# Attention products that read each 128-column tile's two halves alternately, in a fused attention, MoE and GLU kernel

## The chip, the cores and the metric

The kernel runs on one core of a Trainium2 chip. The metric is the device time of one execution in microseconds (us), from the first to the last instruction with what lies around it. The program is one launch: bucketed attention, a top-1 mixture of experts and a gated linear unit follow each other on the same core.

## The reference

Sixteen attention heads (2 batches of 8) have 768 rows of 64 numbers each. A row's bucket is the six signs of its product with `proj`; a query sees only keys of its own bucket.

```python
q_bits = (np.einsum('bhsd,dk->bhsk', q, proj) > 0)      # k_bits likewise; buckets from the bits
mask = q_bucket[:, :, :, None] == k_bucket[:, :, None, :]
scores = np.where(mask, scale * np.matmul(q, k.transpose(0, 1, 3, 2)), -1e9)
attn = np.exp(scores - scores.max(-1, keepdims=True))
out = np.matmul(attn / (attn.sum(-1, keepdims=True) + 1e-9), v)
...
# MoE: each of 1536 rows goes to its best of 8 experts: gate * (relu(x @ w1[e]) @ w2[e])
# GLU: RMS norm, then (silu(xn @ w_gate) * (xn @ w_val)) @ w_out
```

Softmax sums and maxima over keys don't depend on the order in which the keys stand, as long as `v` has the same order. That is what the change uses.

## The kernel before

**Numbers.** Float32 operands are split into a high part `hi` and a rest `lo`, both in a reduced float32 type that TensorE multiplies in one pass. A product is then two or three matmuls into the same PSUM bank.

**Head preparation** (`prep_head`). A head's k and q lie side by side in `kq`, 128 partitions of 6 rows each. Three transposes (`wf`, L501) at a time give 384 columns, from which ScalarE writes `kqh` (L503) and VectorE `kql` (L504). Three sign products (`wp`, L531 to L533) of 384 columns follow; VectorE turns their signs into rows `ft` (L538), and DMAs of the SP queue (`moves`, L495, and L541, L542) put the pieces into the operands `kA`, `kB`, `qA`, `qB`. `kqh` and `kql` exist once (KQ = 1), so that the next head's must wait until these DMAs have read the last head's.

**Units.** A head has 6 units of 128 queries, 96 units in all, numbered `u`. For each unit: `scores` makes `S` (128 queries by 768 keys) in four matmuls of 384 columns (L550, L551); VectorE takes the row maximum (`neg`, L555, and `negm`, L560); ScalarE the exponentials `P` (L569); six transposes put `P` into PSUM tiles `T` (L588, two tiles of 384 columns); ScalarE writes its high part `pth` (L597) and VectorE its rest `ptl` (L598). After three units, `av` multiplies their 384 columns with `v`, 12 matmuls in all (`O`, L619 to L622), spread over the next group's units. `O` is copied out by ScalarE (`osb`, L639) and transposed back by small matmuls (`wo`, L654).

**Order.** The order of the steps is written out by hand: a string of letters (`ORDER`), one letter a step, is run once for each unit; each engine then takes its own instructions in that order. In it `scores(u+2)` comes ahead of `transposes(u)` and of the `av` products, `maxima(u+2)` comes ahead of the two `ptl` of unit `u`. `T`, `wf` and `wp` share three PSUM banks (WB = 3) in turn, `S` has two pairs of banks.

**Reading order.** In the MoE and GLU stages the moving operand of a matmul (the one whose columns stream through the array) is read through `turns`: column 0 of the first half, column 0 of the second half, column 1 of the first, and so on. What is written from those products is sorted back, or their inputs were stored in halves. In attention the moving operand is read column after column. I call these reads turned and plain.

**Loads.** `load_head` issues one DMA for k and one for q from the SP queue (head 0: two each, q's from ScalarE's queue).

Of the kernel before, what the change touches and what calls it, by code (L numbers as in the profile page):

```python
# [14 lines left out]
ALU = mybir.AluOpType  # L15
# [4 lines left out]
P = 128  # L20
# [24 lines left out]
def turns(t):  # L45

    return t.rearrange("p (h a) -> p a h", h=2)


def halves(t):  # L50
# [10 lines left out]
def lsh_attention_moe_glu(  # L61
# [15 lines left out]
    nc = tc.nc  # L77
    B, H, S, D = q.shape
# [5 lines left out]
    T = S // P  # L84
# [3 lines left out]
    HW = 3 * P  # L88
# [113 lines left out]
    for e in range(E):  # L202
        for w_, a_ in ((moe_w1[e], KC), (moe_w2[e], 2)):
            for f in range(F1 // W):
                s_ = w_[:, f * W:(f + 1) * W] if a_ == KC else w_[f * W:(f + 1) * W, :]
# [3 lines left out]
    for f in range(F2 // W):  # L209
        for w_ in (moe2_w_gate, moe2_w_val):  # L210
            s_ = w_.bitcast(I32)[:, 2 * f * W:2 * (f + 1) * W].rearrange("(c p) f -> p c f", p=P)
# [113 lines left out]
    with ExitStack() as ac:  # L325
# [5 lines left out]
        def load_head(n):  # L331
            if n >= NH:
                return
            b, h = divmod(n, H)
            kq = ld.tile([P, T, 2 * D], F32, tag="kq", name=f"kq{n}")
            for j in range(2 if n == 0 else 1):
                ts = slice(3 * j, 3 * j + 3) if n == 0 else slice(0, T)
                for i, src in enumerate((k, q)):
                    eng = nc.scalar if n == 0 and i == 1 else nc.sync
                    eng.dma_start(kq[:, ts, i * D:(i + 1) * D], src[b, h].rearrange("(p t) d -> p t d", t=T)[:, ts])  # L340
            if n == 0:
                for rs in (slice(0, D), slice(D, 2 * D)):
                    nc.sync.dma_start(pr[rs], proj)
            raw[n] = [kq]
            if n != 1:
                load_v(n)
# [83 lines left out]
        vst = {}  # L430
# [39 lines left out]
        def prep_head(n, banks=("w",)):  # L470


            if n >= NH:
                return
            kq = raw[n][0]
            hi = sp.tile([P, S], F32R, tag="kqh", name=f"kqh{n}", bufs=KQ)
            lo = sp.tile([P, S], F32R, tag="kql", name=f"kql{n}", bufs=KQ)
            ft = sp.tile([P, S], F32R, tag="ft", name=f"ft{n}", bufs=1)[0:F]
            bank = {"w": (ps_w, "w"), "0": (ps_w, "w"), "1": (ps_w, "w"), "O": (ps_o, "O")}
            ws = [bank[banks[i % len(banks)]] for i in range(4)]  # L480

            def places():
                for lst, nm in ((kB, "kB"), (qB, "qB")):
                    lst[n] = sp.tile([P, S], F32R, tag=nm, name=f"{nm}{n}")
                for lst, nm in ((kA, "kA"), (qA, "qA")):
                    lst[n] = sp.tile([D + 2 * NB, S], F32R, tag=nm, name=f"{nm}{n}")

            def moves():
                if n > 0:
                    places()  # L490
                lst = [(qA[n][0:D], hi[D:2 * D]), (kB[n][D:2 * D], lo[0:D]), (qB[n][0:D], lo[D:2 * D])]
                if n > 0:
                    lst += [(kA[n][0:D], hi[0:D]), (kB[n][0:D], hi[0:D]), (qB[n][D:2 * D], hi[D:2 * D])]
                for dst, src in lst:
                    nc.sync.dma_start(dst.bitcast(F32), src.bitcast(F32))  # L495

            for j in range(2):
                cs = slice(j * HW, (j + 1) * HW)
                w = ws[j][0].tile([P, 512], F32, tag=ws[j][1], name=f"wf{n}{j}")
                for i in range(3):  # L500
                    nc.tensor.transpose(w[:, i * P:(i + 1) * P], kq[:, 3 * j + i, :], ident)  # L501
                yield
                nc.scalar.activation(hi[:, cs], w[:, 0:HW], AF.Copy, scale=scv)  # L503
                nc.vector.scalar_tensor_tensor(lo[:, cs], w[:, 0:HW], scv, hi[:, cs].bitcast(F32), ALU.mult, ALU.subtract)  # L504
                if n == 0:
                    if j == 0:
                        places()
                    nc.scalar.copy(qB[n][D:2 * D, cs], hi[D:2 * D, cs].bitcast(F32))
                    nc.gpsimd.tensor_scalar(kB[n][0:D, cs], hi[0:D, cs].bitcast(F32), 1.0, 0.0, ALU.mult, ALU.add)
                    if j == 1:  # L510
                        nc.scalar.copy(kA[n][0:D], hi[0:D].bitcast(F32))
                if j == 1 and n < ML:
                    moves()
                yield
            if n == 0:

                rs = slice(D, D + 2 * NB)
                for i, (bk, dst) in enumerate((("1", kA[n]), ("O", kA[n]), ("w", qA[n]), ("0", qA[n]))):
                    j, c0 = i % 2, i // 2 * 32
                    cs = slice(j * HW, (j + 1) * HW)  # L520
                    w = bank[bk][0].tile([P, 512], F32, tag=bank[bk][1], name=f"wp{n}{i}")
                    for i_, (hl, src) in enumerate((("h", hi), ("l", hi), ("h", lo))):
                        nc.tensor.matmul(w[0:rs.stop, 0:HW], pw[hl][:, c0:c0 + rs.stop], src[:, cs], start=i_ == 0, stop=i_ == 2)
                    nc.vector.tensor_scalar(dst[rs, cs], w[rs, 0:HW], 0.0, gam0[rs, i // 2:i // 2 + 1], ALU.is_gt, ALU.subtract)
                    if i < 2:
                        nc.gpsimd.tensor_scalar(dst[rs, cs], dst[rs, cs].bitcast(F32), BIG, 0.0, ALU.mult, ALU.add)
                return
            for j in range(2):
                cs = slice(j * HW, (j + 1) * HW)
                w = ws[2 + j][0].tile([P, 512], F32, tag=ws[2 + j][1], name=f"wp{n}{j}")  # L530
                nc.tensor.matmul(w[0:F, 0:HW], pw["h"][:, D:], hi[:, cs], start=True, stop=False)  # L531
                nc.tensor.matmul(w[0:F, 0:HW], pw["l"][:, D:], hi[:, cs], start=False, stop=False)
                nc.tensor.matmul(w[0:F, 0:HW], pw["h"][:, D:], lo[:, cs], start=False, stop=True)  # L533
                yield
                if j == 0 and n >= ML:

                    moves()
                nc.vector.tensor_scalar(ft[:, cs], w[0:F, 0:HW], 0.0, gam, ALU.is_gt, ALU.subtract)  # L538
                nc.gpsimd.tensor_scalar(ft[0:2 * NB, cs], ft[0:2 * NB, cs].bitcast(F32), BIG, 0.0, ALU.mult, ALU.add)
                if j == 1:  # L540
                    nc.sync.dma_start(qA[n][D:D + 2 * NB].bitcast(F32), ft[32:F].bitcast(F32))  # L541
                    nc.sync.dma_start(kA[n][D:D + 2 * NB].bitcast(F32), ft[0:2 * NB].bitcast(F32))  # L542
                yield

        def scores(u):
            n, t = unit(u)
            s_ = ps_s.tile([P, 2, 512], F32, tag="S", name=f"S{u}")
            for j in range(2):
                cs = slice(j * HW, (j + 1) * HW)
                nc.tensor.matmul(s_[:, j, 0:HW], qA[n][:, t * P:(t + 1) * P], kA[n][:, cs], start=True, stop=False)  # L550
                nc.tensor.matmul(s_[:, j, 0:HW], qB[n][:, t * P:(t + 1) * P], kB[n][:, cs], start=False, stop=True)  # L551
            St[u] = s_

        def maxima(u):
# [47 lines left out]
        def av(g, chunks, t0=0, tn=3):  # L602

            n = order[g][0]
            if tn == 1:

                if t0 == 0:
                    spare.append(ps_s.tile([P, 2, 512], F32, tag="S", name="spare"))
                    Ob[g, t0] = spare[0][:, 0]
                else:  # L610
                    Ob[g, t0] = ps_w.tile([P, 512], F32, tag="w", name=f"O{g}{t0}")
            elif (g, t0) not in Ob:
                Ob[g, t0] = ps_o.tile([P, 512], F32, tag="O", name=f"O{g}")
            hi, lo = PT[g]
            cs = slice(t0 * P, (t0 + tn) * P)
            o = Ob[g, t0]
            for c in chunks:
                if c == 0:
                    nc.tensor.matmul(o[:, cs], vst[n][:, c, :], hi[:, c, cs], start=True, stop=False)  # L619
                nc.tensor.matmul(o[0:D, cs], vst[n][:, c, 0:D], lo[:, c, cs], start=False, stop=False)  # L620
                if c > 0:
                    nc.tensor.matmul(o[:, cs], vst[n][:, c, :], hi[:, c, cs], start=False, stop=c == T - 1)  # L622
            if T - 1 in chunks:
                done.append((g, t0, tn))
                if t0 + tn == 3:
                    PT.pop(g)

        def keep():

            if done:  # L630
# [5 lines left out]
                    o = ld.tile([P, T, 2 * D], F32, tag="kq", name="osbl")[:, 0]  # L636
                else:
                    o = sp.tile([P, HW], F32, tag="osb", name=f"osb{g}{t0}")[:, 0:tn * P]
                nc.scalar.copy(o, Ob.pop((g, t0))[:, t0 * P:(t0 + tn) * P])  # L639
                backs.append(give_back(g, t0, tn, o))  # L640

        def give_back(g, t0, tn, o):
# [711 lines left out]
```

## Time and profile before

| | |
|---|---|
| median of 3 runs | 751.41 us (749.9 to 751.46) |
| the profiled execution's own time | 750.34 us |
| its span, first to last instruction | 748.7 us |
| TensorE busy | 727.0 us, 97% |
| VectorE busy | 596.2 us, 80% |
| ScalarE busy | 375.5 us, 50% |
| GpSimd busy | 256.2 us, 34% |
| attention / MoE / GLU, from their matmuls' starts | to about 271, to about 459, to the end |

An engine is busy while an instruction of its own runs. TensorE's matmuls overlap, and their ends are modelled: a matmul's duration there holds a fixed part of some 0.16 us that the next one hides. What a matmul costs in a stream is therefore read from the distance between two starts, not from its duration.

### The profile page before, as it was taken

How to read it: one execution, taken by the hardware profiler on the slowest of the kernel's cores; microseconds unless marked ns; L12 is line 12 of the kernel's file. 1: busy time of each engine (PE TensorE's matmuls, PEld its weight loads, DVE VectorE, ACT ScalarE, POOL GpSimd, SP SyncE). 2: the span in 40 equal slices, each digit the busy share in tenths (PEclk: the TensorE clock that was granted, in tenths of full speed). 3: DMA queues.
4: the chain of work that ended last, by engine and by line, in shares of the span. 5: the costliest groups of instructions: out<-in, count | busy, mean ns of one | idle time of the engine just before them, and what ended most of it. 6: DMA issues, size and time to landing. Idle time of an engine off the chain costs nothing.

```text
span 748.7 us, 12565 instructions
## 1 busy us (share of the span) xinstructions
PE 727.0 (97%) x4459; PEld 658.1 (88%) x4460; DVE 596.2 (80%) x1094; ACT 375.5 (50%) x777; POOL 256.2 (34%) x434
## 2 busy tenths in 40 slices
PE   8999999999999989999999999999999999999996
PEld 7899999999999889999889888888888888888885
DVE  6999999999999758888798967865777777777633
ACT  5788888888898734345433454433222122211210
POOL 5143444436635543234263422221121121211124
PEclk9999999999999999999999999999999999999999
DMA  7799956555742147577778685422122122210012
GB/s 180 160 267 241 225 133 153 130 146 167 186 108 68 44 131 250 157 228 267 223 229 246 192 281 162 131 59 82 56 57 85 56 62 81 58 56 1 0 57 112
DMA packets 80546, 103.44 MB, mean 138 GB/s; under 512 B 31799, under 2 KB 50231, under 8 KB 80480
## 3 DMA queue, kind: packets, MB, share of 16 engines
q1 hardware_dynamic: 76480, 92.95, 45.1%
q0 software_dynamic: 3200, 9.46, 3.4%
q8 instruction: 36, 0.59, 0.3%
q10 hardware_dynamic: 800, 0.20, 0.1%
q14 instruction: 30, 0.25, 0.1%
HBM read 69.53 MB, written 14.72 MB: 113 GB/s over the span
## 4 chain that ended last, share of the span: by engine, by line
PE 73%; DVE 10%; DMA 4%; issue 4%; ACT 4%; POOL 2%; SPq 1%; POOLq 0%; DVEq 0%; ACTq 0%
PE T L588 8%; DVE lo L275 5%; PE O L620 4%; PE S L550 4%; PE S L551 4%; PE O L622 4%; PE z L1298 4%; PE z L1300 4%; PE z L1299 4%; PE pg L1275 4%; PE pv L1275 4%; PE pg L1276 4%; PE pv L1276 4%; PE pv L1277 4%; PE pg L1277 4%
## 5 line engine op out<-in xcount | busy, mean ns | idle before, releaser
L320 POOL TENSOR_TENSOR wa<-wa,hi 128x512 f32<-128x512 f32 x36 | 58.3, 1619 | 215.4 <-ACT hi L316 209.0
L316 ACT CAST hi<-wa 128x512 fp32r<-128x512 f32 x36 | 22.3, 620 | 162.1 <-DVE wa L314 155.1
L569 ACT ACTIVATE P<-S,negm 128x768 f32<-128x768 f32 x96 | 95.9, 999 | 7.9 <-DVE negm L560 7.1
L598 DVE TENSOR_TENSOR ptl<-T,pth 128x384 fp32r<-128x384 f32 x192 | 97.5, 548 | 1.1 <-ACT pth L597 1.0
L555 DVE TENSOR_REDUCE neg<-S 128x1 f32<-128x768 f32 x96 | 91.0, 948 | 7.8 <-PE S L551 7.3
L597 ACT CAST pth<-T 128x384 fp32r<-128x384 f32 x192 | 82.9, 488 | 7.5 <-PE T L588 5.1
L275 DVE TENSOR_TENSOR lo<-raw,hi 128x1024 fp32r<-128x1024 f32 x58 | 83.8, 1478 | 2.2 <-POOL hi L274 2.2
L588 PE MATMUL T<-ident,P 128*128 128x128 f32 x576 | 79.7, 273 | 0.6 <-ACT rkc L745 0.3
L588 PEld LDWEIGHTS T<-ident,P 128*128 128x128 f32 x576 | 68.6, 141 | 5.4 <-DVE ptl L598 1.4
L550 PE MATMUL S<-kA,qA 76*128 76x384 f32 x192 | 68.3, 356 | 1.9 <-ACT kqh L503 1.3
L551 PE MATMUL S<-kB,qB 128*128 128x384 f32 x192 | 65.3, 340 | 0.4 <-DMA qB<-kql 0.4
L1206 PE MATMUL ph<-xTh,lo 128*128 128x256 f32 x224 | 61.7, 275 | 1.2 <-DVE lo L275 1.2
L1204 PE MATMUL ph<-xTh,hi 128*128 128x256 f32 x224 | 62.8, 280 | 0.0
L620 PE MATMUL O<-ptl,vst 128*64 128x384 f32 (+1 forms) x198 | 62.0, 342 | 0.0
L1205 PE MATMUL ph<-xTl,hi 128*128 128x256 f32 x224 | 61.6, 275 | 0.0
L1280 DVE TENSOR_TENSOR sg<-pv,sg 128x512 f32<-128x512 f32 x36 | 24.7, 686 | 40.6 <-PE pv L1277 40.6
L1275 PE MATMUL pg<-gxh,hi 128*128 128x512 f32 x144 | 54.7, 380 | 0.0
L1298 PE MATMUL z<-hi,hi 128*128 128x512 f32 x144 | 54.7, 380 | 0.0
L1276 PE MATMUL pg<-gxl,hi 128*128 128x512 f32 x144 | 54.6, 379 | 0.0
L1277 PE MATMUL pg<-gxh,lo 128*128 128x512 f32 x144 | 54.6, 379 | 0.0
L1275 PE MATMUL pv<-gxh,hi 128*128 128x512 f32 x144 | 54.6, 379 | 0.0
L1276 PE MATMUL pv<-gxl,hi 128*128 128x512 f32 x144 | 54.6, 379 | 0.0
(236 smaller groups left out, 1952.5 us busy)
## 6 DMA issues: line engine op xcount, KB each, us to landing
raw<-in_moe_w_dram SPq DMA_DIRECT2D x64, 512.0 KB
raw<-in_moe_w_gate_dram SPq DMA_DIRECT2D x12, 512.0 KB
raw<-in_moe_w_val_dram SPq DMA_DIRECT2D x12, 512.0 KB
raw<-in_moe_w_out_dram SPq DMA_DIRECT2D x12, 512.0 KB
xs<-fill SPq DMA_DIRECT2D x16, 257.0 KB
xw<-xs SPq DMA_DIRECT2D x7, 514.0 KB
yt<-yd SPq DMA_DIRECT2D x12, 256.5 KB
v<-in_v_dram SPq DMA_DIRECT2D x16, 192.0 KB
```

The source lines that it names most:

```text
L275: pending.append((i, lambda: (nc.vector.tensor_tensor(lo, r, hi.bitcast(F32), ALU.subtract), load_next())))
L550: nc.tensor.matmul(s_[:, j, 0:HW], qA[n][:, t * P:(t + 1) * P], kA[n][:, cs], start=True, stop=False)
L551: nc.tensor.matmul(s_[:, j, 0:HW], qB[n][:, t * P:(t + 1) * P], kB[n][:, cs], start=False, stop=True)
L555: nc.vector.tensor_reduce(neg[u % 4][:, 1:2], St[u][:, :, 0:HW], AX.XY, ALU.max, negate=True)
L569: nc.scalar.activation(p_, St.pop(u)[:, :, 0:HW], AF.Exp, bias=nm[:, 1:2], scale=nm[:, 0:1], accum_out=sums[n][:, t:t + 1])
L588: nc.tensor.transpose(w[:, c * P:(c + 1) * P], p_[:, j, c * P:(c + 1) * P], ident)
L598: nc.vector.tensor_tensor(lo[:, 3 * j:3 * j + 3, cs], wv, hi[:, 3 * j:3 * j + 3, cs].bitcast(F32), ALU.subtract)
L620: nc.tensor.matmul(o[0:D, cs], vst[n][:, c, 0:D], lo[:, c, cs], start=False, stop=False)
L1275: nc.tensor.matmul(ps_, wh[:, c, fs], turns(xTh[b][:, c]), start=c == 0, stop=False)
L1276: nc.tensor.matmul(ps_, wh[:, c, fs], turns(xTl[b][:, c]), start=False, stop=False)
L1277: nc.tensor.matmul(ps_, wl[:, c, fs], turns(xTh[b][:, c]), start=False, stop=c == KC - 1)
L1298: nc.tensor.matmul(z, hi[:, s_, ts_], turns(oh_[:, s_]), start=s_ == 0, stop=False)
```

## The change

The moving operands of the scores, of the sign products and of the weighted values are read turned within each tile of 128 columns: column `a` of the first 64, then column `a` of the second 64. For the weighted values the columns are queries, so the copy to `osb` sorts them back (it reads PSUM at every second column). For the scores the columns are keys: `S`, `P` and `T` then hold the keys in turned order, and so that this is `v`'s order, k's even rows are loaded into partitions 0 to 63 and its odd rows into 64 to 127, by two DMAs of 64 partitions instead of one of 128. The signs of the sign products are sorted as they are written.

```diff
+def turns_by_tile(t):
+    return t.rearrange("p (c h a) -> p c a h", h=2, a=P // 2)
+def tiles_halves(t):
+    return t.rearrange("p (c h a) -> p c h a", h=2, a=P // 2)
+def tiles_sorted(t):
+    return t.rearrange("p (c a h) -> p c h a", h=2, a=P // 2)
...
                     eng = nc.scalar if n == 0 and i == 1 else nc.sync
+                    if i == 0:
+                        rows = src[b, h].rearrange("(a r t) d -> r a t d", r=2, t=T)
+                        for r in range(2):
+                            eng.dma_start(kq[r * (P // 2):(r + 1) * (P // 2), ts, 0:D], rows[r][:, ts])
+                        continue
                     eng.dma_start(kq[:, ts, i * D:(i + 1) * D], src[b, h].rearrange("(p t) d -> p t d", t=T)[:, ts])
...
-                nc.tensor.matmul(w[0:F, 0:HW], pw["h"][:, D:], hi[:, cs], start=True, stop=False)
+                nc.tensor.matmul(w[0:F, 0:HW], pw["h"][:, D:], turns_by_tile(hi[:, cs]), start=True, stop=False)
...
-                nc.vector.tensor_scalar(ft[:, cs], w[0:F, 0:HW], 0.0, gam, ALU.is_gt, ALU.subtract)
+                nc.vector.tensor_scalar(tiles_halves(ft[:, cs]), tiles_sorted(w[0:F, 0:HW]), 0.0, gam, ALU.is_gt, ALU.subtract)
...
-                nc.tensor.matmul(s_[:, j, 0:HW], qA[n][:, t * P:(t + 1) * P], kA[n][:, cs], start=True, stop=False)
-                nc.tensor.matmul(s_[:, j, 0:HW], qB[n][:, t * P:(t + 1) * P], kB[n][:, cs], start=False, stop=True)
+                nc.tensor.matmul(s_[:, j, 0:HW], qA[n][:, t * P:(t + 1) * P], turns_by_tile(kA[n][:, cs]), start=True, stop=False)
+                nc.tensor.matmul(s_[:, j, 0:HW], qB[n][:, t * P:(t + 1) * P], turns_by_tile(kB[n][:, cs]), start=False, stop=True)
...
-                nc.tensor.matmul(o[0:D, cs], vst[n][:, c, 0:D], lo[:, c, cs], start=False, stop=False)
+                nc.tensor.matmul(o[0:D, cs], vst[n][:, c, 0:D], turns_by_tile(lo[:, c, cs]), start=False, stop=False)
...
-                nc.scalar.copy(o, Ob.pop((g, t0))[:, t0 * P:(t0 + tn) * P])
+                nc.scalar.copy(tiles_halves(o), tiles_sorted(Ob.pop((g, t0))[:, t0 * P:(t0 + tn) * P]))
```

On TensorE, VectorE, ScalarE and GpSimd every instruction keeps its place; only the SP queue gets new rows. Here is the SP queue from the program's start to the end of head 1's moves, before (names are tile<-source; the L numbers are lines of the kernel of before):

```order
L340 DMA kq_93<-in_k_dram 128x3x64 x2
L343 DMA pr<-in_proj_dram 64x6 x2
L351 DMA v_100<-in_v_dram 128x384
L340 DMA kq_164<-in_k_dram 128x6x64
L340 DMA kq_164<-in_q_dram 128x6x64
L495 DMA qA_204<-kqh_192 64x768
L495 DMA kB_201<-kql_193 64x768
L495 DMA qB_202<-kql_193 64x768
L351 DMA v_278<-in_v_dram 128x384
L896 DMA wd<-in_moe_w_gate_dram 64x8x8 x2
L340 DMA kq_285<-in_k_dram 128x6x64
L340 DMA kq_285<-in_q_dram 128x6x64
```

And the same place of the SP queue with the change (its lines are numbered 17 to 19 higher):

```order
L357 DMA kq_93<-in_k_dram 64x3x64 x4
L362 DMA pr<-in_proj_dram 64x6 x2
L370 DMA v_102<-in_v_dram 128x384
L357 DMA kq_166<-in_k_dram 64x6x64 x2
L359 DMA kq_166<-in_q_dram 128x6x64
L514 DMA qA_207<-kqh_195 64x768
L514 DMA kB_204<-kql_196 64x768
L514 DMA qB_205<-kql_196 64x768
L370 DMA v_281<-in_v_dram 128x384
L915 DMA wd<-in_moe_w_gate_dram 64x8x8 x2
L357 DMA kq_288<-in_k_dram 64x6x64 x2
L359 DMA kq_288<-in_q_dram 128x6x64
```

Head 0's k takes two issues more ahead of `proj`, each later head's k one more, and everything behind them in the queue comes that much later.

## Rows read from the trace of the kernel before

**Rows 1.** Windows: PE, PEld, DVE, ACT, POOL busy (count), granted clock, DMA share, GB/s.

```profile
30.00:240.00 210.00, 210.00 (x1481) 196.58 (x1480) 200.59 (x427) 184.26 (x412) 96.95 (x224) 1.00 0.68 171
```

**Rows 2.** Chain of waits from 150 to 175 us, shares by engine and line.

```profile
by line: PE T L588 25.8%; PE S L550 14.5%; PE S L551 14.2%; PE O L620 13.3%; PE O L622 11.3%; PE wo L654 7.5%; PE wp L531 2.8%; PE wp L533 2.8%; PE wp L532 2.7%; PE wf L501 2.6%; PE O L619 2.2%; PE wk L739 0.4%; PE wk L740 0.2%; PE wk L737 
```

**Rows 3.** Timeline of TensorE, plain reads of 384 columns: start, duration, what.

```profile
155.64 0.34 PE L550 MATMUL S<-kA,qA 76*128 76x384 f32 x1
...
156.35 0.82 PE L588 MATMUL T<-ident,P 128*128 128x128 f32 x6
...
157.18 0.33 PE L622 MATMUL O<-pth,vst 128*128 128x384 f32 x1
...
157.87 0.34 PE L622 MATMUL O<-pth,vst 128*128 128x384 f32 x1
```

**Rows 4.** The same view in the GLU stage, turned reads of 512 columns.

```profile
650.00 0.38 PE L1275 MATMUL pg<-gxh,hi 128*128 128x512 f32 x1
...
653.02 0.38 PE L1277 MATMUL pv<-gxh,lo 128*128 128x512 f32 x1
```

**Rows 5.** The same view, 256 columns: plain at 267 us, turned at 276 us.

```profile
267.14 0.40 PE L857 MATMUL xacc<-hot,xl 128*128 128x256 f32 x2
267.38 0.39 PE L857 MATMUL xacc<-hot,ftx 128*128 128x256 f32 x2
...
275.88 0.28 PE L1204 MATMUL ph<-xfhi,hi 128*128 128x256 f32 x1
...
276.88 0.28 PE L1204 MATMUL ph<-xfhi,hi 128*128 128x256 f32 x1
```

**Rows 6.** Groups by line and shape on TensorE: count, busy us, mean ns, idle before.

```profile
L550 PE MATMUL S<-kA,qA 76*128 76x384 f32 x192 | 68.3, 356 | 1.9 <-ACT kqh L503 1.3 <-ACT P L569 0.5
...
L620 PE MATMUL O<-ptl,vst 128*64 128x384 f32 x186 | 60.1, 350 | 0.0
```

**Rows 7.** Timeline of TensorE: one unit's scores, and those six units later.

```profile
114.26 0.42 PE L550 MATMUL S<-kA,qA 76*128 76x384 f32 x1
...
129.61 0.42 PE L550 MATMUL S<-kA,qA 76*128 76x384 f32 x1
```

**Rows 8.** Timeline of VectorE in one unit.

```profile
153.80 0.60 DVE L538 TENSOR_SCALAR ft<-wp,gam 44x384 fp32r<-44x384 f32 x1
154.33 0.94 DVE L555 TENSOR_REDUCE neg<-S 128x1 f32<-128x768 f32 x1
...
155.30 0.16 DVE L560 SCALAR_TENSOR_TENSOR negm<-neg 128x2 f32<-128x2 f32 x1
155.38 1.02 DVE L598 TENSOR_TENSOR ptl<-T,pth 128x384 fp32r<-128x384 f32 x2
```

**Rows 9.** Timelines of VectorE and TensorE where a transpose follows closely on `ptl`.

```profile
160.11 1.02 DVE L598 TENSOR_TENSOR ptl<-T,pth 128x384 fp32r<-128x384 f32 x2
...
161.06 0.82 PE L588 MATMUL T<-ident,P 128*128 128x128 f32 x6
```

**Rows 10.** Groups on ScalarE and VectorE that read PSUM sorted (L1302, L1167) and plain.

```profile
L1279 ACT ACTIVATE sg<-pg 128x512 f32<-128x512 f32 x36 | 21.3, 593 | 19.2 <-PE pg L1277 19.2
...
L1302 ACT COPY acc<-z 128x512 f32<-128x512 f32 x12 | 7.0, 586 | 5.3 <-PE z L1300 5.3
...
L1211 DVE SCALAR_TENSOR_TENSOR hl<-ph,hh 128x512 fp32r<-128x512 f32 x32 | 21.8, 685 | 16.3 <-ACT hh L1210 16.3
...
L1167 DVE TENSOR_TENSOR xTl<-wxw,xTh 128x512 fp32r<-128x512 f32 x14 | 9.6, 687 | 5.6 <-ACT xTh L1166 5.6
```

**Rows 11.** Timeline of the SP queue at the start: start, us of the issue, what.

```profile
4.40 0.65 SPq L340 DMA_DIRECT2D kq<-in_q_dram  x1
6.58 0.54 SPq L495 DMA_DIRECT2D qA<-kqh  x1
```

**Rows 12.** Chain of waits from 20 to 60 us: start, us, what.

```profile
17.14 6.53 DMA qB<-kqh
...
23.74 0.59 ACT kqh L503
```

More of the change, by code (lines that the diff above doesn't have):

```diff
@@ L522, in prep_head @@
                     for i_, (hl, src) in enumerate((("h", hi), ("l", hi), ("h", lo))):
-                        nc.tensor.matmul(w[0:rs.stop, 0:HW], pw[hl][:, c0:c0 + rs.stop], src[:, cs], start=i_ == 0, stop=i_ == 2)
-                    nc.vector.tensor_scalar(dst[rs, cs], w[rs, 0:HW], 0.0, gam0[rs, i // 2:i // 2 + 1], ALU.is_gt, ALU.subtract)
+                        nc.tensor.matmul(w[0:rs.stop, 0:HW], pw[hl][:, c0:c0 + rs.stop], turns_by_tile(src[:, cs]), start=i_ == 0, stop=i_ == 2)
+                    nc.vector.tensor_scalar(tiles_halves(dst[rs, cs]), tiles_sorted(w[rs, 0:HW]), 0.0, gam0[rs, i // 2:i // 2 + 1], ALU.is_gt, ALU.subtract)
                     if i < 2:
@@ L530, in prep_head @@
                 w = ws[2 + j][0].tile([P, 512], F32, tag=ws[2 + j][1], name=f"wp{n}{j}")
-                nc.tensor.matmul(w[0:F, 0:HW], pw["h"][:, D:], hi[:, cs], start=True, stop=False)
-                nc.tensor.matmul(w[0:F, 0:HW], pw["l"][:, D:], hi[:, cs], start=False, stop=False)
-                nc.tensor.matmul(w[0:F, 0:HW], pw["h"][:, D:], lo[:, cs], start=False, stop=True)
+                nc.tensor.matmul(w[0:F, 0:HW], pw["h"][:, D:], turns_by_tile(hi[:, cs]), start=True, stop=False)
+                nc.tensor.matmul(w[0:F, 0:HW], pw["l"][:, D:], turns_by_tile(hi[:, cs]), start=False, stop=False)
+                nc.tensor.matmul(w[0:F, 0:HW], pw["h"][:, D:], turns_by_tile(lo[:, cs]), start=False, stop=True)
                 yield
@@ L618, in av @@
                 if c == 0:
-                    nc.tensor.matmul(o[:, cs], vst[n][:, c, :], hi[:, c, cs], start=True, stop=False)
-                nc.tensor.matmul(o[0:D, cs], vst[n][:, c, 0:D], lo[:, c, cs], start=False, stop=False)
+                    nc.tensor.matmul(o[:, cs], vst[n][:, c, :], turns_by_tile(hi[:, c, cs]), start=True, stop=False)
+                nc.tensor.matmul(o[0:D, cs], vst[n][:, c, 0:D], turns_by_tile(lo[:, c, cs]), start=False, stop=False)
                 if c > 0:
-                    nc.tensor.matmul(o[:, cs], vst[n][:, c, :], hi[:, c, cs], start=False, stop=c == T - 1)
+                    nc.tensor.matmul(o[:, cs], vst[n][:, c, :], turns_by_tile(hi[:, c, cs]), start=False, stop=c == T - 1)
             if T - 1 in chunks:
```

## Prediction

> **What bounds the kernel now.** I read the table by stretches first. From 30 to 240 us, nearly the whole attention stage, TensorE is busy 210.00 of 210.00 us, VectorE 200.59 and ScalarE 184.26, at granted clock 1.00, the 2.4 GHz level [rows 1]. Three engines near full don't tell which one sets the pace, since a busy time holds hidden parts, so the chain of waits comes next: in the steady stage it runs through TensorE alone [rows 2]. No matmul there waits for another engine; each waits for the matmul ahead of it. The scores (L550, L551) have 29% of it, the weighted values (L619, L620, L622) 27%, the sign products (L531 to L533) 8%; the transposes (L588), `wo` and `wf`, some 36%, are not touched by the change. So the stage is worth what the distance between starts is worth. Six units, a head, take 129.61 - 114.26 = 15.35 us [rows 7].
>
> Now the distance itself. Four score matmuls of 384 columns, plain, take 156.35 - 155.64 = 0.71 us, 0.1775 each; four weighted-value matmuls 157.87 - 157.18 = 0.69, 0.1725 each [rows 3]. In the GLU stage 14 turned matmuls of 512 columns take 653.02 - 650.00 = 3.02 us, 0.2157 each [rows 4]. By column that is 0.462 and 0.449 ns plain against 0.421 ns turned, at the same clock. A second pair has one size on both sides, with the same 128 columns of stationary operand: 256 columns plain stand 0.12 us apart (two from 267.14 to 267.38), turned 0.111 (nine from 275.88 to 276.88) [rows 5]. Plain reading is some 7 to 9% slower wherever it is seen here, in the busy middle of attention and in the quiet end of it, so another engine's traffic is not the likely reason.
>
> **The change part by part.**
>
> *The turned reads.* From the 256 and 512 column distances, a turned 384 should cost 0.111 + 128 x (0.2157 - 0.111) / 256 = 0.163 us; by the 512 row alone, 384 x 0.421 = 0.162. These are reads whose halves stand 128 and 256 columns apart. Halves 64 columns apart, as the change has them, are read nowhere in this trace. The price is bounded by 0.162 below; above, by the dearest moving operand that a row shows, the transposes' (below, third rival). I take 0.163, since two distances that differ by a factor of two show the same gain.
>
> I count only what stands after the last stall of the start, from about 24.3 us (23.74 + 0.59 [rows 12]), because before it TensorE waits for data. Scores: the group has 192 on each of two lines, 384 [rows 6]; units 6 to 95 have 360 of them, each 0.0145 cheaper: 5.2 us. Weighted values: 186 full-width ones with `ptl` [rows 6] and as many with `pth`, 372, less some 6 that ran before: 366 x 0.0095 = 3.5 us. Sign products: 14 heads x 6 = 84, taken as weighted values, 0.8 us. Sum 9.5 us. The last products, one tile of 128 columns each, I give nothing.
>
> Here a page speaks against the change. The Trainium skill, "SBUF — State Buffer", section Specifications (TRN2), says that memory lines are 16 bytes, that two hits on a line are needed for full bandwidth and that each crossing to a new line is penalised. A turned read crosses at every column; by this rule the 512-column reads of rows 4 would be the slow ones, and they are the fast ones. For this operand the trace disagrees with the page, and I go by the trace. The skill's "TensorE: Matmul & The Clock Gate", section Back-to-back issue gap, gives columns / 2.4 + 2.5 ns for a lone warm matmul: 215.8 for 512 columns, which rows 4 meet, and 162.5 for 384, which the plain reads of rows 3 miss; by it, an estimate, the sum would be some 9.9 us in place of 9.5.
>
> *The sorted copies.* `osb` and `ft` now read PSUM at every second column. ScalarE's sorted copy of 512 columns takes 586 ns beside 593 for a plain read, VectorE's sorted one 687 beside 685 [rows 10]: nothing, and were it 5%, both engines have that much idle time.
>
> *The loads.* One issue of the SP queue takes 0.65 us [rows 11]. In the steady stage a head's extra issue is hidden by the 15.35 us head for which it is early. At the start it isn't obviously so. Four extra issues come ahead of head 1's moves: two for head 0, one each for heads 1 and 2. The queue is idle from 5.05 to 6.58 us, 1.53 us [rows 11]; three issues, 1.95 us, mostly fit there, and 0.4 us don't. The fourth delays head 1's moves by 0.65. The last of these moves is issued at 17.14 and takes 6.53 us to land, and then `kqh` of head 2 can be written at 23.74 [rows 12]; behind it ScalarE's exponentials queue, and TensorE for them. If the issue time decides, that is 0.4 + 0.65 = 1.1 us on the path; if the transfers ahead of it decide, as 6.53 us for 192 KB suggest, nothing. I take 0.4. `proj` lands two issues later too, and head 0's sign products wait for it; that lies inside the same bounds.
>
> *Where the stall goes.* VectorE is next. Its instructions overlap: a `negm` lasts 0.16 us but the next starts after 0.08 [rows 8], so 0.08 of each is hidden. Then `neg` takes 0.86, `negm` 0.08, two `ptl` 0.94, together 1.88 a unit, 11.3 a head; two `ft` at 0.53 and two `kql`, of the same columns and taken alike, add 2.1 [rows 8]: 13.4 us. TensorE's head goes from 15.35 to 15.35 - 24 x 0.0145 - 30 x 0.0095 = 14.7. VectorE still fits, with 1.3 us left. In detail it is tighter: transposes wait for a bank that the `ptl` two tiles back must have left. At 161 us the pair of `ptl` ends at 161.13 and the second tile's transposes, half of the six that start at 161.06 and take 0.82, start about 161.4 [rows 9]: 0.26 us to spare, of which faster matmuls between take some 0.1. I allow 0.04 us a head, 0.6 in all; nothing below, and 0.3 a head, 4.5 in all, above.
>
> *The sum.* 750.34 - 9.5 + 0.4 + 0.6 = 741.8 us against the profiled execution's own time (its span, 748.7, and 1.6 around it). That execution was 0.4 below the mean of the four times known, 750.78, so I predict 742.2. The MoE and GLU stages only shift: none of their instructions changes.
>
> **The rivals.**
>
> *VectorE takes over.* If the banks leave less room than the average says, transposes wait in every head for 0.3 us. For it: three engines above 87% [rows 1]. Against it: 1.3 us a head left. Time: 742.2 + 4.5 - 0.6 = 746.1, with the worst start 746.8.
>
> *64 columns apart gains nothing.* The gain may hang on the distance. For it: no row has this distance. Against it: 128 and 256 columns gain alike. Time: 750.8, plus a start of 0 to 1.1: 750.8 to 751.9.
>
> *64 columns apart is slow.* If two reads that close collide, a matmul may cost more than a plain one. The dearest moving operand here is the transposes' 128 float32 columns: 0.82 us for six with a hidden part of 0.16, 0.11 each, 0.86 ns a column [rows 9]; 384 columns would take 0.33, and 810 matmuls 0.155 more each: 750.8 + 126 = 876 us. The place is every score and value matmul, and it decides early: from 0.174 a matmul on, 0.0105 above my price, the 8.5 us are gone. That crossing lines is penalised is the page's rule named above; by that rule this is the case that comes.
>
> **How the numbers follow.** About 0.2%, 1.5 us, can be told from no change. Full gain: 0.74, between 738.7 (a turned 384 at 0.162 saves 10.3 us, nothing is lost, and if weighted values stand as far apart as scores now, 366 x 0.005 = 1.8 more) and 744. VectorE takes over: 0.11. No gain: 0.09. Slow: 0.06. The predicted time is the first's. The range takes in the second and leaves out 0.15: 738.7 to 747. Faster 0.85, same 0.09, slower 0.06.
>
> **What would show it right or wrong.** In the changed kernel's timeline four scores should take 0.65 us in place of 0.71, and a head 14.7 in place of 15.35; the chain of waits should still run through TensorE alone in the middle, with `ptl` named now and then before transposes; `osb` and `ft` should keep their mean; the first scores after the start's stall should come at 24.5 to 25.5. I am wrong if scores stand 0.17 or more apart, if idle time before L588's counterpart grows beyond some 2 us with VectorE as its releaser, or if the start loses more than 1.1 us.

## The result and the profile after

The changed kernel takes 744.63 us (median; 743.26 to 744.9) beside 751.31 us for the kernel before (749.9 to 751.46): ratio 0.9913, 95% interval 0.9899 to 0.9927, so 6.7 us faster. The profiled execution took 744.9 us with a span of 742.9, against 750.34 and 748.7. In the code of the changed kernel the scores are L569 and L570, the transposes L607, the weighted values L638 to L641, the sign products L550 to L552, `pth` L616, `ptl` L617, `neg` L574, `negm` L579.

The window over the attention stage, as in [rows 1] (busy time and count of PE, PEld, DVE, ACT, POOL; granted clock; DMA share; GB/s):

```profile
30.00:240.00 210.00, 209.12 (x1523) 196.73 (x1522) 205.09 (x442) 188.90 (x424) 98.71 (x228) 1.00 0.67 171
```

TensorE is no longer busy throughout: 0.88 us are missing, and VectorE has gone from 200.59 to 205.09, since the same 210 us now hold more tiles. The granted clock is 1.00 as before. Then the matmuls themselves, on TensorE's timeline (start, duration, what):

```profile
72.89 0.33 PE L641 MATMUL O<-pth,vst 128*128 128x384 f32 x1
...
73.70 0.33 PE L550 MATMUL wp<-kqh,pwh 128*44 128x384 f32 x1
...
74.19 0.33 PE L569 MATMUL S<-kA,qA 76*128 76x384 f32 x1
...
74.86 0.82 PE L607 MATMUL T<-ident,P 128*128 128x128 f32 x6
```

Five weighted-value matmuls take 73.70 - 72.89 = 0.81 us, 0.162 each; three sign products 0.49, 0.163 each; four scores 0.67, 0.1675 each, where the plain ones of [rows 3] stood at 0.1775. Averaged over the starts from 100 to 230 us, weighted values went from 0.175 (not the 0.1725 of the stretch in [rows 3]) to 0.1625, scores from 0.1775 to 0.166. The head of [rows 7] goes from 15.35 to 14.90 us, not to 14.7. To see where the rest is, I follow the first scores matmul of a tile through the stage. Before:

```profile
24.50 0.41 PE L550 MATMUL S<-kA,qA 76*128 76x384 f32 x1 [1.25 <-ACT kqh L503]
...
68.18 0.42 PE L550 MATMUL S<-kA,qA 76*128 76x384 f32 x1
...
70.93 0.42 PE L550 MATMUL S<-kA,qA 76*128 76x384 f32 x1
...
251.28 0.44 PE L550 MATMUL S<-kA,qA 76*128 76x384 f32 x1
```

The same four tiles after, and one head of the middle (the rows at 113.23 and 128.13):

```profile
25.12 0.41 PE L569 MATMUL S<-kA,qA 76*128 76x384 f32 x1
...
67.44 0.41 PE L569 MATMUL S<-kA,qA 76*128 76x384 f32 x1
...
71.34 0.40 PE L569 MATMUL S<-kA,qA 76*128 76x384 f32 x1 [0.88 <-DMA xs<-fill]
...
113.23 0.41 PE L569 MATMUL S<-kA,qA 76*128 76x384 f32 x1
...
128.13 0.41 PE L569 MATMUL S<-kA,qA 76*128 76x384 f32 x1
...
245.76 0.43 PE L569 MATMUL S<-kA,qA 76*128 76x384 f32 x1 [0.22 <-ACT P L588]
```

After the start the changed kernel is 0.62 us late; by the end of head 3 it is 0.74 ahead; one tile on it is 0.41 late again, a step of 1.15 us; at the last tile it is 5.52 ahead. From the start to the last tile the gain is 6.14 us, against 9.5 - 0.6 = 8.9 in the sum. Two waits of TensorE between 30 and 240 us, read on its weight loads (PEld), stand for the difference (engine, line, waited for; us in total, times, longest):

```profile
PEld T L607 <- DVE ptl L617: 1.6, 10, 0.2
PEld S L569 <- ACT kqh L522: 1.1, 1, 1.1
```

The first are ten waits of 0.15 to 0.2 us for `ptl`, all behind the stop at 71.34. The second is the stop before 71.34: the weight load's row names `kqh`, the matmul's own row a DMA, and e5 and the landings of the DMAs decide between them. The experiments take the start, the 71.34 stop and the `ptl` waits one by one.

### The profile page after: what moved, and what is told of

It reads as the page before. It is cut to its first block, busy times and chain, and to the rows that moved or that the text cites. A ratio compares the mean times of both kernels' runs of the same rounds, so it can differ in the third digit from the quotient of the medians.

```text
span 742.9 us, 12599 instructions
## 1 busy us (share of the span) xinstructions
PE 720.8 (97%) x4459; PEld 653.4 (88%) x4460; DVE 594.6 (80%) x1094; ACT 375.0 (50%) x777; POOL 254.6 (34%) x434
## 4 chain that ended last, share of the span: by engine, by line
PE 63%; DVE 15%; DMA 8%; issue 5%; ACT 4%; POOL 3%; SPq 2%; POOLq 0%; DVEq 0%; ACTq 0%
PE T L607 7%; DVE lo L288 5%; PE z L1317 4%; PE z L1319 4%; PE z L1318 4%; PE pv L1295 4%; PE pg L1295 4%; PE pg L1296 4%; PE pv L1296 4%; PE pg L1294 4%; PE pv L1294 4%; PE S L569 3%; PE O L639 3%; PE S L570 3%; PE O L641 3%
## 5 line engine op out<-in xcount | busy, mean ns | idle before, releaser
L617 DVE TENSOR_TENSOR ptl<-T,pth 128x384 fp32r<-128x384 f32 x192 | 97.3, 547 | 1.5 <-ACT pth L616 0.8
L574 DVE TENSOR_REDUCE neg<-S 128x1 f32<-128x768 f32 x96 | 90.8, 946 | 2.9 <-PE S L570 2.4
L616 ACT CAST pth<-T 128x384 fp32r<-128x384 f32 x192 | 83.2, 488 | 3.0 <-PE T L607 2.2
L607 PE MATMUL T<-ident,P 128*128 128x128 f32 x576 | 81.5, 275 | 0.9 <-DVE ptl L617 0.5
L607 PEld LDWEIGHTS T<-ident,P 128*128 128x128 f32 x576 | 67.8, 141 | 7.0 <-DVE ptl L617 3.2
L569 PE MATMUL S<-kA,qA 76*128 76x384 f32 x192 | 66.2, 345 | 1.8 <-ACT P L588 0.9
L570 PE MATMUL S<-kB,qB 128*128 128x384 f32 x192 | 63.0, 328 | 0.6 <-DMA qB<-kql 0.6
L639 PE MATMUL O<-ptl,vst 128*64 128x384 f32 (+1 forms) x198 | 59.8, 332 | 0.0
```

The source lines that it names most:

```text
L574: nc.vector.tensor_reduce(neg[u % 4][:, 1:2], St[u][:, :, 0:HW], AX.XY, ALU.max, negate=True)
L607: nc.tensor.transpose(w[:, c * P:(c + 1) * P], p_[:, j, c * P:(c + 1) * P], ident)
L616: nc.scalar.copy(hi[:, 3 * j:3 * j + 3, cs], wv)
L617: nc.vector.tensor_tensor(lo[:, 3 * j:3 * j + 3, cs], wv, hi[:, 3 * j:3 * j + 3, cs].bitcast(F32), ALU.subtract)
```

## The experiments

Medians of different chips differ by some us, so each run goes by its ratio to the kernel before on the same chip, and by where in its trace a tile starts.

**e1, the loads alone.** The kernel before, with `k` in two DMAs and every read plain.

```
 eng = nc.scalar if n == 0 and i == 1 else nc.sync
+if i == 0:
+    rows = src[b, h].rearrange("(r a t) d -> r a t d", r=2, t=T)
+    for r in range(2):
+        eng.dma_start(kq[r * (P // 2):(r + 1) * (P // 2), ts, 0:D], rows[r][:, ts])
+    continue
```

> The kernel before, all reads plain, with only k's load cut into two DMAs of 64 partitions (two halves in order, so nothing else changes). Theory: the extra issues cost at the start only; there the first five units come some 2 us later, as in the changed kernel, and the stall at head 2's preparation swallows most of it, so 0.4 to 1.2 us in all: 751.7 to 752.5 against 751.3. Rival (the extra DMAs cost in every head, and are the whole of the lost gain): 754 or more.

Measured: 751.34 us, ratio 1.0012 (0.9996 to 1.0029); span 749.2 against 748.7. The SP queue at the start, before (first row) and in this run, and TensorE's first scores in this run:

```profile
0.84 0.98 SPq L340 DMA_DIRECT2D kq<-in_k_dram  x2
...
0.84 2.77 SPq L343 DMA_DIRECT2D kq<-in_k_dram  x4
...
5.57 1.22 SPq L343 DMA_DIRECT2D kq<-in_k_dram  x2
```

```profile
12.24 0.43 PE L555 MATMUL S<-kA,qA 76*128 76x384 f32 x1
...
25.35 0.42 PE L555 MATMUL S<-kA,qA 76*128 76x384 f32 x1
```

The four issues for head 0 fill 2.77 us where two took 0.98. The queue is busy almost without a gap up to the first moves at 7.57 us, where it had 1.53 us to spare before; the first scores start 2 us late (10.28 before), and the stall that follows before 24.5 us takes up all but 0.85 of it (25.35 against 24.50). The tiles behind it keep that lag to within 0.1 us to the last tile of attention: in the steady stage the extra issue costs nothing, as predicted. The median's ratio can't tell the 0.85 us from nothing.

**e3, the turned reads without the extra DMAs.** `k` comes by one DMA as before; in its place the rows of `v` are permuted within their own single DMA, so that sums over the keys come in one order.

```
-    for r in range(2):
-        eng.dma_start(kq[r * (P // 2):(r + 1) * (P // 2), ts, 0:D], rows[r][:, ts])
...
-nc.sync.dma_start(t, v[b, h].rearrange("(p t) d -> p t d", t=T))
+nc.sync.dma_start(t, v[b, h].rearrange("(r a t) d -> a r t d", r=2, t=T))
```

> The changed kernel with k loaded by one DMA as before; instead v, in one DMA as well, puts row block a and row block 64 + a into partitions 2a and 2a + 1, so that keys and values agree. All turned reads, no extra DMA. Theory: the start's 0.6 us come back, but the wait at head 4's first scores, for operands that land behind the fills, takes part of it: 743 to 744.5. Rival (all lost gain comes from the extra DMAs): 741.5 to 742.

Measured: 743.4 us, ratio 0.9902 (0.9875 to 0.993). The start loses nothing (the tile of 24.50 starts at 24.27), but the span of the profiled execution (745.09 us), 743.4, is no better than the 742.9 of the change, because head 4 starts at 71.63 although head 3's last tile starts at 67.19; the 0.29 us by which head 4 is later there than in the change are also what the last tile is later. So the stop at head 4 is not made by the extra DMAs.

**e4, the weighted values alone.** The kernel before, with L638 to L641 turned and `osb` sorted, scores and sign products plain.

```
-nc.tensor.matmul(o[0:D, cs], vst[n][:, c, 0:D], lo[:, c, cs], start=False, stop=False)
+nc.tensor.matmul(o[0:D, cs], vst[n][:, c, 0:D], turns_by_tile(lo[:, c, cs]), start=False, stop=False)
...
-nc.scalar.copy(o, Ob.pop((g, t0))[:, t0 * P:(t0 + tn) * P])
+nc.scalar.copy(tiles_halves(o), tiles_sorted(Ob.pop((g, t0))[:, t0 * P:(t0 + tn) * P]))
```

> The kernel before with only the weighted values turned and osb sorted back; scores, sign products and loads as before. Theory: 372 matmuls go from about 0.175 to 0.163 apart, 4.6 us, less some 0.5 for VectorE: 747 to 747.5 us. Scores stay 0.177 apart. Rival (VectorE eats what TensorE gives from the first microsecond on): above 749.

Measured: 746.24 us, ratio 0.9937 (0.9914 to 0.996). A head of the middle takes 128.59 - 113.54 = 15.05 us:

```profile
113.54 0.42 PE L563 MATMUL S<-kA,qA 76*128 76x384 f32 x1
...
128.59 0.42 PE L563 MATMUL S<-kA,qA 76*128 76x384 f32 x1
```

That is 0.30 under the 15.35 of [rows 7]. Only the 24 weighted values of a head are turned here, so each saves 0.30 / 24 = 0.0125 us, a third more than the 0.0095 of the prediction, by which they would have saved 0.23. In this kernel head 4 starts at 70.79, before the change at 70.93, in e3 at 71.63, in the change at 71.34: it doesn't come forward, though head 3's last tile starts between 67.19 and 68.18.

**e5, the fills two heads later.** The changed kernel; the DMAs that fill the routed rows (`xs<-fill`, 257 KB each) are issued in heads 3 to 6 instead of 1 to 4.

```
-if t in (2, 5) and n > 0 and 2 * (n - 1) + t // 3 < E:
-    fill_windows(2 * (n - 1) + t // 3)
+if t in (2, 5) and n >= 3 and 2 * (n - 3) + t // 3 < E:
+    fill_windows(2 * (n - 3) + t // 3)
```

> The changed kernel, with the 16 fills of the expert windows issued in heads 3 to 6 instead of 1 to 4. Theory: the wait of head 4's first scores on its sign rows (1.2 us, they land behind fills) goes: 743.4 to 743.8 us against 744.6 of the changed kernel. Rival (the wait comes from the extra k DMAs or from the eight transfers in flight, whatever they are): unchanged within 0.3.

Measured: 743.86 us, ratio 0.9909 (0.9881 to 0.9936): the median does not part it from the change. The traces do: the window from 60 to 72 us of the changed kernel,

```profile
60.00:72.00 12.00, 11.12 (x79) 10.11 (x78) 11.21 (x24) 10.41 (x24) 6.08 (x14) 1.00 1.01 248
```

and of e5:

```profile
60.00:72.00 12.00, 12.00 (x89) 11.30 (x89) 11.73 (x25) 10.63 (x24) 6.30 (x15) 1.00 0.54 150
```

In the first the DMA engines' share is 1.01 and TensorE misses 0.88 us; in the second it is 0.54 and TensorE misses nothing, head 4 starts at 70.34, and the last tile starts 0.77 us earlier than in the change. What head 4 waits for can be read from the SP queue and the chain of the changed kernel:

```profile
62.54 1.22 SPq L161 DMA_DIRECT2D xs<-fill  x2
64.12 0.81 SPq L560 DMA_DIRECT2D qA<-ft  x1
65.04 0.78 SPq L561 DMA_DIRECT2D kA<-ft  x1
65.87 1.15 SPq L161 DMA_DIRECT2D xs<-fill  x2
```

```profile
60.62 6.05 DMA kA<-kqh
...
66.69 4.53 DMA xs<-fill
...
71.34 0.40 PE S L569
```

The scores read no filled row; they need `kA` and `qA` with their sign rows, whose DMAs are issued at 64.12 and 65.04 behind two fills, while the engines are full. The chain names a fill, but the trace also holds the moments at which each DMA's parts report in, and these settle it: in the change the last parts of `qA<-ft` and `kA<-ft` land at 71.02 and 71.20, and the scores start at 71.34. In e5 `kA<-ft` lands at 65.58, 2.3 us after its issue in place of 6.2. In e7 (below), where the stop falls at 72.33, the matmul's own row names the same DMA, which lands there at 72.19:

```profile
72.33 0.40 PE L569 MATMUL S<-kA,qA 76*128 76x384 f32 x1 [0.95 <-DMA kA<-ft]
```

The start of head 4 is therefore set by the DMA engines once attention gets there early enough.

**e6, VectorE relieved.** The changed kernel with the row maxima over half of the keys.

```
-nc.vector.tensor_reduce(neg[u % 4][:, 1:2], St[u][:, :, 0:HW], AX.XY, ALU.max, negate=True)
+nc.vector.tensor_reduce(neg[u % 4][:, 1:2], St[u][:, 0, 0:HW], AX.X, ALU.max, negate=True)
```

> The changed kernel, with VectorE's row maxima of every scores tile taken over the first half of the keys alone (384 columns instead of 768; rows whose largest score lies in the other half get another shift, so this leaves out half of the maximum). Theory: where a head of the changed kernel takes 14.9 us instead of 14.7, TensorE waits for the ptl subtractions, because VectorE's column of work is nearly as long as TensorE's; with some 0.4 us less of it per tile the waits of the T transposes on ptl go, every full head takes 14.7 us, and the median is about 2 us under the changed kernel's, some 742.4. Rival: those waits are set by ScalarE's or by the banks' order and stay; then the median stays at 744.4 to 744.9.

**e7, no low parts from GpSimd.**

```
-nc.gpsimd.tensor_tensor(lo[:, cs], r[:, cs], hi[:, cs].bitcast(F32), ALU.subtract)
+nc.gpsimd.tensor_scalar(lo[:, cs], hi[:, cs].bitcast(F32), 0.0, 0.0, ALU.mult, ALU.add)
```

> The changed kernel, with the weights' low parts that GpSimd subtracts in heads 2 and later (lo<-raw,hi, 0.73 us each, two tensors read) written as zeros by a one-source multiplication of hi; the output lacks these low parts. VectorE has the same instructions. Theory: the heads with a wait for ptl are those in which the two-tensor subtraction on GpSimd stretches a negm of VectorE from 0.16 to about 0.5 us and so puts ptl later; without it no negm is stretched beside these steps and the T waits of those heads go: a gain of 0.2 us in some ten heads, to about 742.5 to 743.5. Rival: the stretch only coincides, and VectorE is late from its own load alone: no change of the median beyond 0.3 us and the same T waits.

Measured: e6 742.72 us, ratio 0.9877 (0.9853 to 0.9902); e7 744.17, ratio 0.99 (0.9875 to 0.9924). e6 came out as expected: its head 4 starts 1.28 us later than in the change, since its first heads take longer (why is open), and from there on it makes up 1.67 us. e7's median missed, but its waits did not: between 100 and 240 us the changed kernel has

```profile
PEld T L607 <- DVE ptl L617: 1.3, 8, 0.2
```

and e7

```profile
PEld T L607 <- DVE ptl L617: 0.2, 1, 0.2
```

and e6 none. (The stop at head 4 lies ahead of this window.) One head of the middle, first e6, then e7:

```profile
116.68 0.41 PE L569 MATMUL S<-kA,qA 76*128 76x384 f32 x1
...
131.37 0.41 PE L569 MATMUL S<-kA,qA 76*128 76x384 f32 x1
```

```profile
116.39 0.41 PE L569 MATMUL S<-kA,qA 76*128 76x384 f32 x1
...
131.08 0.41 PE L569 MATMUL S<-kA,qA 76*128 76x384 f32 x1
```

14.69 us in both, the 14.7 of the prediction. Why the low parts cost TensorE time is on the timeline of the changed kernel:

```profile
120.55 0.73 POOL L301 TENSOR_TENSOR lo<-raw,hi 128x256 fp32r<-128x256 f32 x1
...
120.78 0.52 DVE L579 SCALAR_TENSOR_TENSOR negm<-neg 128x2 f32<-128x2 f32 x1
...
121.22 1.01 DVE L617 TENSOR_TENSOR ptl<-T,pth 128x384 fp32r<-128x384 f32 x2
...
122.28 0.31 PEld L607 LDWEIGHTS T<-ident,P 128*128 128x128 f32 x3 [0.15 <-DVE ptl L617]
```

`negm`, 0.16 us elsewhere, lasts until 121.30, GpSimd's subtraction until 121.28; `ptl` comes later by that much, and the transposes of the second half wait for it. Seven of the ten waits follow such a `negm`; two more, at 173.55 and 174.02, follow the longest, which another subtraction of GpSimd holds, that of the low part of `v` (it ends at 173.01, `negm` at 173.03):

```profile
172.00 1.01 POOL L486 TENSOR_TENSOR vst<-v,vst 128x384 fp32r<-128x384 f32 x1
...
172.41 0.62 DVE L579 SCALAR_TENSOR_TENSOR negm<-neg 128x2 f32<-128x2 f32 x1
```

e7 keeps that subtraction, but the two fall otherwise there, and its longest `negm` is 0.375. A `negm` stretched in the same way (0.51 us at 121.95) is in the trace of before, where TensorE came late enough not to notice. The Trainium skill, "SBUF — State Buffer", section SBUF: two separate sides, says that VectorE and GpSimd share one port pair under an exclusive lock, held for a whole instruction, and that a VectorE operation with two SBUF inputs contends with GpSimd's reads; `negm` reads two such inputs and ends with GpSimd's instruction, so the trace agrees.

In e7's profiled execution (745.27 us) head 4 starts at 72.33, 1 us later than in the change; from that tile to the last it is 1.58 us faster. `kA<-ft` is issued 1.4 us later there, at 66.41; I don't know why, nor whether the other executions, which set the median, had the same stop.

**e8, the distance between the alternate columns.** The kernel before with the weighted values turned at a distance set by head.

```
+DIST = {n: d for n, d in zip(range(3, 15), (32, 32, 16, 16, 8, 8, 4, 4, 2, 2, 1, 1))}
+def turned(d, t):
+    return t.rearrange("p (c h a) -> p c a h", h=2, a=d)
...
-nc.tensor.matmul(o[0:D, cs], vst[n][:, c, 0:D], lo[:, c, cs], start=False, stop=False)
+nc.tensor.matmul(o[0:D, cs], vst[n][:, c, 0:D], turned(DIST.get(n, 64), lo[:, c, cs]), start=False, stop=False)
```

> The kernel before, with the weighted values alone turned, and the distance between the two columns that are read alternately set by head: 64 columns as in the change, but 32 in heads 3 and 4, 16 in heads 5 and 6, 8 in 7 and 8, 4 in 9 and 10, 2 in 11 and 12, and 1 (a plain read) in 13 and 14; the copy that sorts them follows. Theory, from the 384 columns that the expert layers' turned reads have between their pairs and the 64 of the change, both 0.163 us for 384 columns: any distance that keeps neighbours in time out of one aligned group of a few columns gives 0.163, so 32 and 16 do for certain, and the step grows to the plain 0.172 to 0.176 only at 4, 2 or 1. Rival: the gain grows with the distance and 32 already shows a step between 0.163 and 0.175.

Measured: 748.54 us (one execution). Five steps at a distance of 4 columns, then five at 2:

```profile
171.23 0.33 PE L643 MATMUL O<-pth,vst 128*128 128x384 f32 x1
...
172.04 0.34 PE L571 MATMUL S<-kA,qA 76*128 76x384 f32 x1
```

```profile
201.75 0.33 PE L643 MATMUL O<-pth,vst 128*128 128x384 f32 x1
...
202.61 0.34 PE L571 MATMUL S<-kA,qA 76*128 76x384 f32 x1
```

At 4 columns 0.81 / 5 = 0.162 us, as at every larger distance of this run; at 2 columns 0.86 / 5 = 0.172, as plain (averaged over their heads 0.1625 and 0.175). The gain is whole or absent, and the edge lies between halves 16 bytes apart (4 columns) and 8 bytes. The theory held, though the turned reads that it starts from stand 128 and 256 columns apart, not 384; 64 columns are far more than needed.

**e9, no extra DMAs and the fills later** (e3 and e5 together).

> The change without its extra DMAs and with the window fills later: k loaded by one DMA as before, scores still turned, v's rows permuted in its own one DMA instead, and the fills of the routed rows in heads 3 to 6 instead of 1 to 4. Theory: the start's loss (0.6 to 0.8 us) and the stop at head 4 (1.15 us) are both gone and nothing else moves, so 1.8 us under the changed kernel, near 742.8. Rival: the fills later collide with weights that the expert layer waits for, or v's permuted load has shorter pieces and takes its place, and it comes out within 0.5 us of the changed kernel.

Measured: 743.42 us, ratio 0.9889 (0.9869 to 0.9909), span 741.7. Both early losses are gone in the trace: the tile of 25.12 starts at 24.07, that of 71.34 at 69.08. That is 2.26 us; 2.0 of them are left at the last tile, and 1.2 at the end of the kernel (more on that below). So the 1.8 us of the forecast are there in attention and not in the span, and the ratio's interval overlaps with that of the change.

**e10, the low parts in quarters.** e9 with

```
-nc.gpsimd.tensor_tensor(lo[:, cs], r[:, cs], hi[:, cs].bitcast(F32), ALU.subtract)
+for d in range(0, 256, 64):
+    ds = slice(c * 256 + d, c * 256 + d + 64)
+    nc.gpsimd.tensor_tensor(lo[:, ds], r[:, ds], hi[:, ds].bitcast(F32), ALU.subtract)
```

> The kernel of the run e9 (k by one DMA, v's rows permuted in its one DMA, fills of the routed rows two heads later), with each two-tensor subtraction of the weights' low parts on GpSimd cut in four of 64 columns; the same values are computed. Theory: a VectorE instruction that meets the subtraction is held at most to the end of the piece that runs, some 0.2 to 0.25 us instead of up to 0.5, so ptl comes in time, the eight T waits of 0.2 us between 100 and 250 us go, full heads are 14.7 us, and the median is some 1.2 to 1.6 us under e9. Rival: four short pieces hold VectorE as long in sum as one long, since each takes the port anew, or the extra fixed cost on GpSimd makes other work late: no gain.

Measured: 741.55 us, ratio 0.9892 (0.9877 to 0.9907), span 740.7, the shortest of all. The waits of the transposes between 30 and 240 us fall from 13 to

```profile
PEld T L603 <- DVE ptl L613: 0.3, 2, 0.2
```

and where the last head starts attention is 1.5 us ahead of e9; at the last tile 1.2 are left, at the end of the kernel 1.0. The ratios can't part e10 from e9 (the forecast's 1.2 to 1.6 us don't show in them); the waits can. These subtractions grow from 17 x 0.73 to 68 x 0.32 us between 100 and 240 us, and no wait of TensorE for them shows.

**e11, `ptl` ahead of the maxima.** e9 with the steps of a tile in another order.

```
-ORDER = "opqESTAFmvrnHf"
+ORDER = "opqESTAFHmvrnf"
```

> The kernel of the run e9 with the parts of the transposed tiles (pth, ptl) written in each tile's step ahead of the row maxima and shifts of the tile two further on, instead of behind them. Theory: if ptl alone is late, VectorE doing it first takes the T waits of the stalled heads away, and the maxima have room: about 1.2 us under e9. Rival: the pth copy that ptl needs waits behind ScalarE's exponential, so that VectorE sits idle before ptl and neg and negm come later; then ScalarE's exponential waits for negm, a tile takes longer, and the kernel is slower than e9.

Measured: 855.61 us, ratio 1.1416 (1.14 to 1.1432). The rival held, and by far more than a wait's size. Its waits from 100 to 240 us:

```profile
ACT P L582 <- DVE negm L573: 58.2, 39, 1.8
DVE ptl L611 <- ACT pth L610: 45.5, 38, 1.6
PEld S L563 <- ACT P L582: 28.5, 37, 1.4
```

`ptl` waits for `pth`, which stands behind the exponential `P` on ScalarE; `P` waits for `negm`, which now stands behind `ptl` on VectorE. The two engines take turns, a tile takes 3.66 us, and TensorE waits for both.

**e12, control.** The kernel before with e6's half maxima.

> Control for e6: the kernel before, with the row maxima over the first half of the keys alone (which leaves out half of each maximum). Theory: before the change TensorE had so much work in a tile that VectorE's column was covered, so a relief of 0.4 us per tile gains nothing in the middle heads (100 to 230 us), which stay at 15.2 to 15.35 us each. Rival: VectorE's load delayed TensorE before too, and these heads shorten by 0.2 us or more, as they did in e6.

Measured: 752.43 us (one execution), span 750.8. A head of the middle:

```profile
119.45 0.42 PE L550 MATMUL S<-kA,qA 76*128 76x384 f32 x1
...
134.79 0.42 PE L550 MATMUL S<-kA,qA 76*128 76x384 f32 x1
```

15.34 us, as in [rows 7]. What gave 0.2 us a head after the change gave nothing before it: the wait on VectorE is one that the change laid bare. (The longer span comes from the first heads: head 4 starts at 73.50.)

## Why the prediction was right, and where it was off

The forecast was 742.2 us with 738.7 to 747; it came out at 744.63, faster by 0.9%. Read by the profiled execution, 741.8 was summed and 744.9 came. The mechanism was right, but the range held in part by luck: 744.63 lies just above the 744 that the full gain was given, and inside the range only because that reached on to the second rival. That rival isn't what came; a stop that no case held and a VectorE term sized too small are.

**The turned reads, 9.5 us: right as a sum, by two misses that cancel.** Where nothing else holds TensorE, a head takes 14.69 us (e6, e7) beside the 14.7 worked out, that is 0.65 less than before. Weighted values and sign products stand at the 0.162 to 0.163 that was interpolated from 256 and 512 columns. Scores reach only 0.166 on average (0.1675 in the tile above), not 0.163: 360 x 0.0115 = 4.1 us in place of 5.2. Weighted values make that good, since plain ones stood 0.175 apart on average and not the 0.1725 of the four in [rows 3]: 366 x 0.0125 = 4.6 us in place of 3.5, as e4's head shows too. Each score matmul has a full 128-column stationary operand, as half of the weighted values do; what holds the scores I didn't try. At 64 columns the gain is as at 128 and 256: the two rivals on the distance fall, and e8 shows that a distance of 2 columns would have been the one without a gain. The rule of the Trainium skill ("SBUF — State Buffer", section Specifications (TRN2)) that each crossing to a new 16-byte line is penalised is at odds with e8: the reads that cross at every column are the fast ones.

**The start, 0.4 us: measured 0.62 in the changed kernel and 0.85 with the loads alone (e1).** The ends of 0 and 1.1 held. The reading that three issues mostly fit into the queue's idle 1.53 us was wrong: the first scores come 2.05 us late, and it is the stall before 24.5 us that absorbs most of it.

**The extra issue in the steady stage, nothing: right** (e1).

**VectorE and the banks, 0.6 us: too small.** This is the term that was mis-sized most. From the stop at head 4 to the last tile, e7 and e6 beat the change by 1.58 us and 1.67. The step said that 0.26 us were to spare between `ptl` and the transposes; it took that from one tile in which `negm` lasted 0.16 us. In tiles where a subtraction of GpSimd meets `negm` the spare time is smaller by up to 0.46 us, and in these the transposes wait. It is no rival's takeover (0.3 us in every head; e7's gain is 0.2 to 0.3 us in seven of heads 4 to 14 and next to nothing in the other four), but it is the same place. In heads 1 to 3 the change gains 1.36 us over 17 tiles where 17 x 0.65 / 6 = 1.84 was to be had. What took these 0.5 us is not shown: no wait of more than 0.15 us stands there, and head 2 takes 14.86 us in e10 and 14.87 in e7 too.

**Left out of the sum: the stop at head 4, 1.15 us.** The prediction said that the stages behind attention only shift; it did not ask what else shares the DMA engines when attention comes earlier. From 55 to 70 us their share was 1.09 before the change too, only no one waited for them: `kA<-ft` landed at 70.40 there, and head 4 started at 70.93.

```profile
55.00:70.00 15.00, 15.00 (x108) 14.10 (x107) 14.36 (x31) 13.20 (x29) 6.40 (x16) 1.00 1.09 271
```

Together: 9.5 - 0.6 (the start) - 1.15 (the stop) - 1.6 (VectorE) - 0.5 (heads 1 to 3) = 5.65 us, beside 5.52 at the last tile and 5.72 at the end of the span.

**The sorted copies: nothing, right.** `osb` stays at 480 ns a copy (481 before) and `ft` at 599 (600):

```profile
L557 DVE TENSOR_SCALAR ft<-wp,gam 44x384 fp32r<-44x384 f32 x30 | 17.9, 599 | 0.1
...
L658 ACT COPY osb<-O 128x384 f32<-128x384 f32 x31 | 14.9, 480 | 8.3 <-PE O L641 8.3
```

**Still open.** Gains of attention partly vanish in its last head and behind it: e10's lead of 1.5 us over e9 is 1.2 at the last tile and 1.0 at the end, e9's of 2.0 over the change 1.2. Between the expert layer's matmuls TensorE waits longer for the weights' `lo` after the change, 2.1 us in place of 1.2 at one line, but the total by which each kernel loses there differs from run to run, and no run isolates it. The medians of e3, e5, e9 and e10 can't be ranked: their intervals overlap with each other and with that of the change.

## What to carry to other kernels

The price of a turned read, taken from other stages of the same trace, held to 3% here. The price of a plain one, taken from four matmuls, was 1.5% too low, and that made the gain, a small difference of two prices, a quarter too small; take both prices as a mean over many rows. What went missing was where faster work arrived at things that had been just in time: a shared DMA queue, an instruction on another engine that now and then takes three times as long. So ask of each stage what its slack is in the worst tile, not in a typical one, and look for the largest duration in a group, not only its mean. And before reordering two engines' work to shorten a wait of 0.2 us, follow the ring of waits through both: e11's span is 114 us longer than e9's for such a swap.

## What the runs showed of the hardware

At granted clock 1.00, TensorE's moving operand in the reduced float32 type, read at alternate columns 4 to 64 apart, costs 0.162 to 0.163 us for 384 columns (weighted values, e8); read plain or at a distance of 2, 0.172 to 0.1775; scores are the exception, with 0.166 to 0.1675 turned. A two-tensor subtraction of GpSimd holds a `negm` of VectorE to its own end, 0.52 us instead of 0.16. With the subtraction cut in pieces of 64 columns (e10, the row below: shortest, middle and longest in ns), a `negm` beside it took 0.345 us at most; the longest, 0.371, stands beside another instruction of GpSimd (`xs`).

```profile
L575 DVE SCALAR_TENSOR_TENSOR negm<-neg x57: 123/161/371, 101.0 to 237.5; 128x2 f32<-128x2 f32 x57
```
